# Decode attention with a long cache: keys turned in place on VectorE, block-diagonal query weights, exp before the turn of the scores, shared weight loads, fixed engine orders

## The chip, the cores and the metric

One core of one Trainium2 chip runs the whole program. The metric is the device time of one execution in microseconds (us), lower is better. Every execution that is compared below is marked fast in the record. Where times are compared, the kernels ran in the same rounds on the same chip, unless the text says that they are of different calls.

## The reference, cut to what matters

One token goes through a pre-norm block: attention over a cache of 65,536 positions with 32 query heads on 4 key/value heads, and then a gated MLP.

```python
def _A_ref(x, k_cache, v_cache, wq, wo):        # x [1,1,1024], caches [1,4,65536,128], bf16
    q = (x @ wq).reshape(B, 1, 32, 128).transpose(0, 2, 1, 3)
    k = jnp.repeat(k_cache, 8, axis=1); v = jnp.repeat(v_cache, 8, axis=1)
    p = softmax(einsum("bhqd,bhkd->bhqk", q, k) * 128 ** -0.5)
    return einsum("bhqk,bhkd->bhqd", p, v).transpose(0, 2, 1, 3).reshape(B, 1, 4096) @ wo
h  = x + _A_ref(layernorm(x), k_cache, v_cache, wq, wo)
h2 = h + (gelu(n @ w_gate) * (n @ w_up)) @ w_down      # n = layernorm(h); [1024,3584], [3584,1024]
```

Keys and values are 67 MB each and the weights 39 MB. Every byte is read once, so this is a program that loads.

## The kernel before

All large loads go through one queue into five buffers of 4 MB (32 KB in each of 128 partitions), in the order wq, K of head 0, then K of head g+1 and V of head g in turn, wo, gate, up, and the down weights in pieces of 14, 7, 4, 2 and 1 columns of 256 KB.

```python
    CW = 16384; NBUF = 5
    chpool = ctx.enter_context(tc.tile_pool(name="chpool", bufs=NBUF))
    def load(src, name):
        t = chpool.tile([P, CW], BF16, name=name, tag="ch")
        ...
        nc.sync.dma_start(out=tv, in_=src)
```

A key position lies in one partition, but the score matmul needs the 128 elements of a key across partitions. So TensorE turns pairs of bf16 as fp32 words, 128 by 128 at a time, and VectorE and ScalarE copy the result out of PSUM in turn:

```python
    # k_chunk_T, for each block b of four in a bank
    nc.tensor.transpose(out=kt_ps[:, b, :], in_=k32s[m0 // 16][:, m0 % 16, :], identity=ident_f[:])
    ...
    if act_for(g, ci, c): nc.scalar.copy(out=dst_bf, in_=src_bf)
    else:                 nc.vector.tensor_copy(out=dst_bf, in_=src_bf)
    # k_chunk_QK: four matmuls side by side on strips of 32 array columns
    for par in range(2):
        for c in range(4):
            nc.tensor.matmul(qk_ps[32 * c:32 * c + 32, :], lhsT=qsel[:, g, par, hf, :],
                             rhs=mv[:, :, 32 * c:32 * c + 32, par], ..., tile_position=(0, 32 * c))
```

The first 14 of the 28 columns of the down weights give rows in PSUM. Two neighbouring columns, each in two halves, use the four strips. The rows are copied out and summed over strips by fp32 matmuls ("row sum" below). The other 14 columns run as small matmuls with one output column, which can follow the last loads closely:

```python
    def pair_mm(bank, stat, w2, c, first, last):
        for s in range(DS):                       # two halves of 512
            g = 2 * s + c % 2
            nc.tensor.matmul(bank[32 * g:32 * g + 32, :], lhsT=stat, rhs=w2[:, s * 512:(s + 1) * 512], ...)
    def cp_sum(row, add, name):                   # the row sum: 4 fp32 matmuls
        for b in range(4):
            nc.tensor.matmul(ps[:, b, :], lhsT=row[:, b * P:(b + 1) * P], rhs=hsel[:], start=True, stop=True)
    sizes = [14, 7, 4, 2, 1]; NW = sizes[0]
    for sz in sizes:
        wv = load(wd_v[:, c0:c0 + sz, :], "wd_sb")
        for cc in range(sz):
            c = c0 + cc
            if c < NW:
                pair_mm(d_ps, actz[:, c, :], wv[:, cc, :], c, c < 2, c + 2 >= NW); continue
            for j in range(DC):
                nc.tensor.matmul(dl_ps[:, j:j + 1], lhsT=wv[:, cc, j * P:(j + 1) * P], rhs=act_bf[:, c:c + 1], ...)
        c0 += sz
        if c0 == NW: ...                          # evacuation to d_r, then cp_sum(d_r)
```

## Time and profile before

| | before |
|---|---|
| time, median of 4 (range) | 411.93 us (411.78 to 412.08) |
| span of the profiled run | 410.2 us |
| read from HBM | 173.0 MB |
| busy: PE (TensorE matmul), PEld (weight load), DVE (VectorE), ACT (ScalarE) | 66%, 47%, 41%, 40% |
| the load queue's share of 16 DMA engines' span | 98.1% |

These are lines of the profile's page of the kernel before. In the first two, busy time, share of the span and number of instructions are given by engine. The DMA row has the busy tenths of 40 equal slices of the span, and below it stands what they moved. Then come two DMA queues (packets, MB, share) and groups of instructions (busy us, mean ns of one, idle time of the engine before them, and what ended most of it).

```profile
span 410.2 us, 5998 instructions
...
PE 271.7 (66%) x2577; PEld 193.1 (47%) x2577; DVE 168.9 (41%) x292; ACT 162.9 (40%) x249; POOL 5.1 (1%) x16
...
DMA  8999999999999999999999999999999999999993
GB/s 358 412 457 407 457 408 449 419 439 428 430 436 428 439 417 451 411 449 415 447 421 439 425 428 439 427 441 427 441 424 441 428 433 425 433 441 411 446 415 163
...
q1 hardware_dynamic: 6496, 173.02, 98.1%
q8 instruction: 20, 0.33, 0.3%
...
L216 PE MATMUL kt_ps<-ident_f,k_sb 128*128 128x128 f32 x1024 | 144.5, 304 | 37.4 <-DMA k_sb<-in_A_k_cache_dram 34.4
L216 PEld LDWEIGHTS kt_ps<-ident_f,k_sb 128*128 128x128 f32 x1024 | 131.6, 158 | 58.1 <-issue 36.6
L220 ACT COPY kt_sb<-kt_ps 128x1024 bf16<-128x1024 bf16 x116 | 111.9, 1016 | 105.5 <-issue 74.8
L222 DVE COPY kt_sb<-kt_ps 128x1024 bf16<-128x1024 bf16 x140 | 95.3, 688 | 92.9 <-PE kt_ps L216 89.7
...
```

The DMA row stands at its highest digit from the second slice to the last but one. The most expensive groups all belong to the turn of the keys. There is a second queue, of kind "instruction", with 0.3%: the program's own instructions.

The next lines are of the timeline of the same run at its end (start us, duration, engine, line, operation, tiles, count, and in brackets the idle time before and its releaser). `d_ps` are the row matmuls, `hd_cp_ps` is the row sum, `dl_ps` are the small matmuls.

```profile
...
398.42 2.66 PE L353 MATMUL d_ps<-wd_sb,actz 128*32 128x512 bf16 x28 [2.72 <-DMA wd_sb<-in_B_w_down_dram]
...
401.13 0.69 DVE L461 COPY d_r<-d_ps 128x512 f32<-128x512 f32 x1 [5.20 <-PE d_ps L353]
...
401.87 1.87 PE L382 MATMUL hd_cp_ps<-hsel,d_r 128*128 128x2 f32 x8 [0.79 <-DVE d_r L461]
...
403.60 2.50 PE L456 MATMUL dl_ps<-act_bf,wd_sb 128*128 128x1 bf16 x88
...
406.32 1.01 PE L456 MATMUL dl_ps<-act_bf,wd_sb 128*128 128x1 bf16 x24 [0.21 <-DMA wd_sb<-in_B_w_down_dram]
407.37 0.17 DVE L463 TENSOR_TENSOR o_col<-dl_ps,hd_cp 128x8 bf16<-128x8 f32 x1 [3.41 <-PE dl_ps L456]
...
408.18 0.36 SPq L468 DMA_DIRECT2D out_dram<-o_row  x1
...
```

The last small matmuls wait for the last load, and the transfer of the output starts 0.85 us after they end.

### The profile page before, as it was taken

What the parts mean: (1) busy time and instruction counts of PE and PEld (TensorE: products, weight loads), DVE (VectorE), ACT (ScalarE), POOL (GpSimd) and SP (SyncE); (2) the same over time, 40 slices, a digit from 0 to 9 for tenths busy, and PEclk for the clock granted to TensorE, in tenths of its full rate; (3) what the DMA queues carried; (4) which work ended last, traced back from release to release, by engine and by line L of the source; (5) the groups of instructions that cost most, each with busy time, mean ns of one, the idle gap of its engine ahead of it and who ended that gap; (6) DMA issues with size and microseconds to landing.
All of it is one profiled execution on the core that took longest, in us unless ns stands there. A gap on an engine that the chain in (4) does not pass through costs nothing.

```text
span 410.2 us, 5998 instructions
## 1 busy us (share of the span) xinstructions
PE 271.7 (66%) x2577; PEld 193.1 (47%) x2577; DVE 168.9 (41%) x292; ACT 162.9 (40%) x249; POOL 5.1 (1%) x16
## 2 busy tenths in 40 slices
PE   0448888797994938964858399394945526467266
PEld 0227666484673727644555277182822213163135
DVE  0213787766772636751727086344630001022011
ACT  0014676597570648641525775152638000000000
POOL 1000000000000000000000000000020000000000
PEclk9986999969998886996969689979875655557665
DMA  8999999999999999999999999999999999999993
GB/s 358 412 457 407 457 408 449 419 439 428 430 436 428 439 417 451 411 449 415 447 421 439 425 428 439 427 441 427 441 424 441 428 433 425 433 441 411 446 415 163
DMA packets 6682, 173.40 MB, mean 423 GB/s; under 512 B 896, under 2 KB 896, under 8 KB 1152
## 3 DMA queue, kind: packets, MB, share of 16 engines
q1 hardware_dynamic: 6496, 173.02, 98.1%
q8 instruction: 20, 0.33, 0.3%
q14 instruction: 6, 0.05, 0.0%
q10 hardware_dynamic: 160, 0.00, 0.0%
HBM read 173.02 MB, written 0.00 MB: 422 GB/s over the span
## 4 chain that ended last, share of the span: by engine, by line
DMA 51%; PE 21%; ACT 6%; DVE 4%; issue 2%; DVEq 0%
DMA k_sb<-in_A_k_cache_dram 27%; PE kt_ps L216 13%; DMA wo_sb<-in_A_wo_dram 11%; DMA wu_sb<-in_B_w_up_dram 10%; ACT pT L272 4%; DMA wd_sb<-in_B_w_down_dram 3%; PE qk_ps L239 3%; ACT kt_sb L220 2%; PE acc_ps L289 2%; DVE mx L246 1%; PE at_ps L353 1%; PE wu_ps L158 1%; DVE kt_sb L222 1%; DVE sc_sb L245 1%; PE o_ps L305 1%
## 5 line engine op out<-in xcount | busy, mean ns | idle before, releaser
L216 PE MATMUL kt_ps<-ident_f,k_sb 128*128 128x128 f32 x1024 | 144.5, 304 | 37.4 <-DMA k_sb<-in_A_k_cache_dram 34.4
L216 PEld LDWEIGHTS kt_ps<-ident_f,k_sb 128*128 128x128 f32 x1024 | 131.6, 158 | 58.1 <-issue 36.6
L220 ACT COPY kt_sb<-kt_ps 128x1024 bf16<-128x1024 bf16 x116 | 111.9, 1016 | 105.5 <-issue 74.8
L222 DVE COPY kt_sb<-kt_ps 128x1024 bf16<-128x1024 bf16 x140 | 95.3, 688 | 92.9 <-PE kt_ps L216 89.7
L272 ACT ACTIVATE pT<-sc_sb,nbias 128x256 bf16<-128x256 f32 x64 | 47.5, 746 | 23.7 <-DVE nbias L264 23.7
L239 PE MATMUL qk_ps<-kt_sb,qsel 128*32 128x512 bf16 x512 | 39.6, 384 | 9.9 <-ACT kt_sb L220 9.2
L289 PE MATMUL acc_ps<-v_sb,pT 128*32 128x512 bf16 x512 | 37.4, 441 | 12.2 <-DMA v_sb<-in_A_v_cache_dram 12.2
L246 DVE TENSOR_REDUCE mx<-sc_sb 128x8 f32<-128x512 f32 x32 | 35.2, 1100 | 0.5
L245 DVE STREAM_TRANSPOSE sc_sb<-qk_ps 128x512 f32<-128x512 f32 x32 | 23.0, 717 | 19.0 <-PE qk_ps L239 18.7
L289 PEld LDWEIGHTS <-pT 128*32 128x32 bf16 x512 | 16.8, 107 | 28.9 <-issue 19.9
L165 ACT COPY wg_ev<-wg_ps 96x512 f32<-96x512 f32 x1 | 0.6, 582 | 59.4 <-PE wg_ps L158 59.4
L239 PEld LDWEIGHTS <-qsel 128*32 128x32 bf16 x512 | 8.3, 94 | 24.5 <-DVE kt_sb L222 15.2
L298 PE MATMUL l_ps<-lpart,ones_f 128*128 128x8 f32 x16 | 3.8, 312 | 21.7 <-ACT pT L272 21.7
L298 PEld LDWEIGHTS l_ps<-lpart,ones_f 128*128 128x128 f32 x16 | 3.2, 249 | 23.9 <-ACT pT L272 23.1
L158 PEld LDWEIGHTS <-hnz 128*32 128x32 bf16 x112 | 5.0, 127 | 17.6 <-issue 15.6
L158 PE MATMUL wu_ps<-wu_sb,hnz 128*32 128x512 bf16 x56 | 6.6, 579 | 9.3 <-DMA wu_sb<-in_B_w_up_dram 9.3
L353 PE MATMUL at_ps<-wo_sb,o2z 128*32 128x512 bf16 x64 | 7.2, 630 | 8.3 <-DMA wo_sb<-in_A_wo_dram 8.3
L272 ACT ACTIVATION_READ_ACCUMULATOR pT<-sc_sb,nbias 128x1 f32 x64 | 12.1, 190 | 0.0
L302 DVE COPY acc_sb<-acc_ps 128x512 f32<-128x512 f32 x4 | 2.7, 684 | 22.7 <-PE acc_ps L289 22.7
L165 ACT ACT_TABLE_LOAD x1 | 1.3, 1283 | 25.8 <-DVE q_ev L163 25.8
L125 PE MATMUL ln_tot<-ln_s,ones_f 128*128 128x1 f32 x4 | 1.2, 363 | 13.9 <-DVE ln_s L123 13.9
L353 PEld LDWEIGHTS <-o2z 128*32 128x32 bf16 x64 | 2.7, 140 | 12.0 <-issue 11.5
(108 smaller groups left out, 93.0 us busy)
## 6 DMA issues: line engine op xcount, KB each, us to landing
k_sb<-in_A_k_cache_dram SPq DMA_DIRECT2D x16, 4096.0 KB, 40.2
v_sb<-in_A_v_cache_dram SPq DMA_DIRECT2D x16, 4096.0 KB, 37.5
wq_sb<-in_A_wq_dram SPq DMA_DIRECT2D x2, 4096.0 KB, 16.8
wo_sb<-in_A_wo_dram SPq DMA_DIRECT2D x2, 4096.0 KB, 43.3
wg_sb<-in_B_w_gate_dram SPq DMA_DIRECT2D x2, 3584.0 KB, 43.7
wu_sb<-in_B_w_up_dram SPq DMA_DIRECT2D x2, 3584.0 KB, 40.6
wd_sb<-in_B_w_down_dram SPq DMA_DIRECT2D x1, 3584.0 KB
wd_sb<-in_B_w_down_dram SPq DMA_DIRECT2D x1, 1792.0 KB, 29.6
```

The source lines that it names most:

```text
L158: nc.tensor.matmul(banks[s // 4][32 * g:32 * g + 32, :], lhsT=stat, rhs=mov(s), start=first, stop=last, tile_position=(0, 32 * g))
L216: nc.tensor.transpose(out=kt_ps[:, b, :], in_=k32s[m0 // 16][:, m0 % 16, :], identity=ident_f[:])
L220: nc.scalar.copy(out=dst_bf, in_=src_bf)
L222: nc.vector.tensor_copy(out=dst_bf, in_=src_bf)
L239: nc.tensor.matmul(qk_ps[32 * c:32 * c + 32, :], lhsT=qsel[:, g, par, hf, :], rhs=mv[:, :, 32 * c:32 * c + 32, par], start=(hf == 0 and pa ...
L245: nc.vector.transpose(out=sl.rearrange("p n h -> p (n h)"), in_=qk_ps[:])
L246: nc.vector.tensor_reduce(out=st["mx"][:, :, pi], in_=sl.rearrange("p n h -> p h n"), axis=AX.X, op=ALU.max)
L272: nc.scalar.activation(out=pT[:, :, r, :], in_=sc_sb[:, hf * HG * TG:(hf + 1) * HG * TG, r].rearrange("p (a t) -> p a t", t=TG), func=ACT. ...
L289: nc.tensor.matmul(acc[32 * c:32 * c + rep * TG, :], lhsT=pTs[a // HG][:, a % HG, :, :].rearrange("p r t -> p (r t)"), rhs=v_sb[:, i * TG: ...
L298: nc.tensor.matmul(l_ps[:], lhsT=ones_f[:], rhs=lpart[:, hf, :], start=(hf == 0), stop=(hf == NH - 1))
L305: nc.tensor.matmul(o_ps[:], lhsT=acc_sb[:, t * Dh:(t + 1) * Dh], rhs=sel[:, t:rep * TG:TG], start=(t == 0), stop=(t == TG - 1))
L353: nc.tensor.matmul(bank[32 * g:32 * g + 32, :], lhsT=stat, rhs=w2[:, s * 512:(s + 1) * 512], start=first, stop=last, tile_position=(0, 32 ...
```

## The change

Its intent is to take TensorE, VectorE and ScalarE out of the way of the loads. VectorE turns each K load in place in blocks of 32x32 words. Query weights are laid out block-diagonally with zeros, so that TensorE scores the half-turned keys directly with the whole array. Exp runs on rows of scores that are contiguous, and only the probabilities are turned. Matmuls that use the same weights as the one before them drop the second weight load. Fixed orders on each engine take the place of the scheduler's choice. In the output stage, gate and up alternate, both halves of a column use the same strip and so share a weight load, and 21 columns instead of 14 of the down weights give rows. Buffers, load sizes and bytes are unchanged. The core of the diff, with cuts:

```diff
+    def k_load(g, li):
+        kt = kv_load(k_v[g], li, "k_sb").rearrange("p n d -> p (n d)").bitcast(U32)
+        for c in range(NSP):                                   # NSP = 4, w = 2048 words
+            dv(nc.vector.transpose(out=kt[:, c * w:(c + 1) * w], in_=kt[:, c * w:(c + 1) * w]))
...
+        for a in range(TG):
+            for bp in range(4):
+                o = W0 + (g * 4 + bp) * P - a * rep
+                for k in range(2):
+                    mm(qk_ps[:, k, :], wsel[:, o:o + P], kt[:, a, k, :, bp // 2, :, bp % 2],
+                       a == 0 and bp == 0, a == TG - 1 and bp == 3, loaded=(k == 1))
...
-                nc.tensor.transpose(out=kt_ps[:, b, :], in_=k32s[m0 // 16][:, m0 % 16, :], identity=ident_f[:])
...
+            ac(nc.scalar.activation(out=pe_r[:], in_=state.pop(("sc", g, li))[:], func=ACT.Exp, ...))
+            dv(nc.vector.transpose(out=pT[:].rearrange("p m c -> p (m c)"), in_=pe_r[:]))
...
+    def row_mm(banks, stat, w2, c, first, last):
+        g = c % 4
+        for s in range(DS):
+            mm(banks[s][32 * g:32 * g + 32, :], stat, w2[:, s * 512:(s + 1) * 512], first, last,
+               loaded=(s > 0), tile_position=(0, 32 * g))
...
     def cp_sum(row, add, name):
         for b in range(4):
-            nc.tensor.matmul(ps[:, b, :], lhsT=row[:, b * P:(b + 1) * P], rhs=hsel[:], start=True, stop=True)
+            for s in range(DS):
+                mm(ps[:, b, s:s + 1], row[:, s, b * P:(b + 1) * P], ones_f[:, 0:1], True, True)
...
-    NW = sizes[0]
+    NW = 21
```

## The prediction

> **What bounds it now.** The DMA stream. The page counts 173.0 MB read from HBM; the DMA row of the 40 slices reads 9 (90% or more busy) from the second slice to the next to last; the queue table gives the load queue 98.1% of 16 engines' span. Windows of 10 us move about 420 to 465 GB/s whatever the engines do: 426 at 310-320 us with PE busy 7.6 of 10, 419 at 330-340 with PE at 3.5 and VectorE idle. The Trainium skill ("DMA: Bandwidth & Descriptors", Specifications) gives a fabric ceiling of 435 GB/s; the trace agrees, about 431 sustained. PE (66%), VectorE (41%) and ScalarE (40%) have slack. The chain of waits shows 51% DMA and 21% PE, but its PE pieces run beside a full queue: loads are issued 40.2 us (K) before they land, at 9.7 us of stream per 4 MB load (estimate: 4.19 MB at 431 GB/s). Only the end is exposed: the last weights land near 406.95 us, the span ends at 410.2.
>
> **What the change does.** It takes out 1024 fp32 PE transposes (144.5 us busy), 256 evacuations (95.3 us VectorE, 111.9 ScalarE) and strided exps (47.5 us). It adds 64 in-place turns of 128x2048 words. Estimate: the 128x512 stream transpose takes 717 ns, so about 1.05 ns per element plus 0.18 us: 2.3 us each, 9.3 per K load. Scores and values become 512 + 512 matmuls of 512 columns on the whole array, about 0.215 us each at full clock (timeline starts), 0.427 at half: 6.9 or 13.7 us per load. Estimated busy: PE 250 us, PEld under 70, VectorE 190-200, ScalarE 40-50. Per K+V pair (19.4 us of stream) VectorE needs 11-13 us, PE 13.8; in the first head, K alone, VectorE needs about 10.5 per 9.7, which five buffers absorb. All this is off the critical path; bytes, load sizes and buffers are unchanged. Fewer instructions spare instruction fetch (0.3% of queue time): at most 0.5 us.
>
> **The end gets longer.** Before, the 14-column piece of the down weights lands at 398.4; 28 matmuls run in fours on different column strips (2.66 us), the row sum ends at 403.7, and 88+24 small matmuls follow the data. Now 21 columns go this way, and both halves of a column use one strip: about 15 slots of 0.215-0.427 us (3.2-6 us), then 8 more for the 7-column piece (estimated to land at 402.7), evacuation 0.7, row sum 1-2, then 56 small matmuls (26.7 ns apart, 1.5 us). PE then ends between 408 and 411 instead of 407.3.
>
> **Prediction.** 411.87, minus 0.3, plus 0.6 to 3.5: about 412.9 us, 80% range 411.0 to 415.5. Faster by over 2%: 2%; within 2%: 94%; slower by over 2%: 4%.
>
> **What would show it.** DMA row still 9s, load queue about 98%, same rate; last load landing within 1 us of before; K turns near 2.3 us; the last small matmuls waiting for PE, not for the last load; 4-6 us between last landing and end (3.3 before).
>
> **What would make it wrong.** Turns at two cycles per element (18 us per load) would make VectorE the bound: tens of us slower. PE held at half clock would need 27 us per pair. In-place turns could slow the DMA's writes; the skill ("SBUF — State Buffer", Who interferes with whom) says DMA ports are separate from the engines', which the constant rate supports. If the tail's small matmuls still hide behind the data, the time is 411.5.

## The result and the profile after

| | before | after |
|---|---|---|
| time, median of 4 (range) | 411.93 us (411.78 to 412.08) | 410.84 us (410.12 to 411.24) |
| span of the profiled run | 410.2 us | 409.5 us |
| last load has landed | 406.91 us | 404.18 us |
| from there to the end of the span | 3.3 us | 5.3 us |
| matmuls + weight loads on TensorE | 5154 | 2253 |

The ratio is 0.9969, 95% interval 0.9955 to 0.9983. It and all ratios below are from the fast runs of the same rounds; they are not quite the quotients of the quoted medians. The time lies 0.16 us below the low end of the predicted range: the change gave a small gain, clear of noise, where a small loss was forecast.

The lines of the page after that answer to those of before:

```profile
span 409.5 us, 2725 instructions
...
PE 307.7 (75%) x1521; PEld 70.6 (17%) x732; DVE 202.6 (49%) x189; ACT 45.5 (11%) x68; POOL 7.2 (2%) x17
...
DMA  8999999999999999999999999999999999999993
GB/s 359 410 461 410 453 416 442 427 439 432 415 451 416 455 411 451 419 448 423 439 431 426 445 414 450 419 445 423 448 423 434 435 426 445 419 432 429 439 413 151
...
q1 hardware_dynamic: 6496, 173.02, 98.1%
q8 instruction: 9, 0.15, 0.1%
...
L259 DVE STREAM_TRANSPOSE k_sb<-k_sb 128x2048 uint32<-128x2048 uint32 x64 | 142.1, 2278 | 33.8 <-DMA k_sb<-in_A_k_cache_dram 33.8
L127 PE MATMUL qk_ps<-k_sb,wsel 128*128 128x512 bf16 x256 | 104.7, 409 | 37.5 <-DVE k_sb L259 25.2
L129 PE MATMUL acc_ps<-v_sb,pT 128*128 128x512 bf16 x384 | 111.3, 401 | 0.0
...
```

The attention did what it was meant to do. The turns of the keys take 2278 ns each, weight loads fall from 193 to 71 us, ScalarE from 163 to 45 us. The load queue's share is 98.1% as before, so none of this was on the path. But the instruction queue has 9 packets instead of 20.

The end of the timeline after, with the row matmuls, the evacuation, the row sum, the small matmuls and the output:

```profile
...
395.65 0.62 PE L127 MATMUL d_ps<-wd_sb,actz 128*32 128x512 bf16 x4 [3.10 <-DMA wd_sb<-in_B_w_down_dram]
...
396.03 0.67 PE L129 MATMUL d_ps<-wd_sb,actz 128*32 128x512 bf16 x4
...
399.89 0.41 PE L127 MATMUL d_ps<-wd_sb,actz 128*32 128x512 bf16 x4 [0.91 <-DMA wd_sb<-in_B_w_down_dram]
...
400.98 0.69 DVE L216 COPY d_r<-d_ps 128x512 f32<-128x512 f32 x1 [7.95 <-PE d_ps L129]
...
401.72 3.36 PE L127 MATMUL hd_cp_ps<-ones_f,d_r 128*128 128x1 f32 x16 [0.79 <-DVE d_r L216]
...
404.95 1.63 PE L127 MATMUL dl_ps<-act_bf,wd_sb 128*128 128x1 bf16 x56
...
406.62 0.17 DVE L529 TENSOR_TENSOR o_col<-dl_ps,hd_cp 128x8 bf16<-128x8 f32 x1 [1.32 <-PE dl_ps L127]
...
407.44 0.37 SPq L534 DMA_DIRECT2D out_dram<-o_row  x1
...
```

The row matmuls start 2.8 us earlier than before: the 14-column piece was awaited until 395.65 us instead of 398.42. But now the 7-column piece gives rows too and is awaited until 399.89 us, so the evacuation starts only 0.15 us earlier (400.98 instead of 401.13). Then the row sum takes 3.36 us instead of 1.87. The small matmuls come after it in one go (the last load landed at 404.18, before they began). The end of the chain is only 0.7 us earlier.

So the question is why the loads end 2.7 us earlier, when neither their rate nor their number changed.

**Where the loads ended.** The first view is of the windows at the end of the run before: the stretch, its length, then PE, PEld, DVE, ACT and POOL busy, the granted clock, and last the DMA engines' mean busy share and GB/s.

```profile
...
402.00:403.00 1.00, 1.00 (x6) 1.00 (x6) 0.00 (x0) 0.00 (x0) 0.00 (x0) 0.50 0.70 291
403.00:404.00 1.00, 1.00 (x19) 1.00 (x20) 0.17 (x1) 0.00 (x0) 0.00 (x0) 0.50 0.54 221
404.00:405.00 1.00, 1.00 (x44) 1.00 (x42) 0.00 (x0) 0.00 (x0) 0.00 (x0) 0.50 0.55 219
405.00:406.00 1.00, 1.00 (x41) 1.00 (x38) 0.00 (x0) 0.00 (x0) 0.00 (x0) 0.50 0.27 92
406.00:407.00 1.00, 0.74 (x21) 0.57 (x19) 0.00 (x0) 0.00 (x0) 0.00 (x0) 0.50 0.08 29
...
```

The same view after:

```profile
...
402.00:403.00 1.00, 1.00 (x6) 1.00 (x7) 0.00 (x0) 0.00 (x0) 0.00 (x0) 0.50 0.68 272
403.00:404.00 1.00, 1.00 (x6) 1.00 (x6) 0.00 (x0) 0.00 (x0) 0.00 (x0) 0.50 0.34 131
404.00:405.00 1.00, 1.00 (x8) 1.00 (x8) 0.00 (x0) 0.00 (x0) 0.00 (x0) 0.50 0.00 0
405.00:406.00 1.00, 1.00 (x41) 1.00 (x41) 0.17 (x1) 0.00 (x0) 0.00 (x0) 0.50 0.00 0
...
```

Up to 402 us both run at full rate (shares of 0.97 to 1.03 in the windows from 398 us, not printed). At 402-403 us both fall to about 0.7. Before, some engines then go on for four more microseconds, with a share of about half until 405; after, they have all but stopped by 404. This is not a faster stream. It is a stream whose engines finish closer together.

The Trainium skill says in "DMA: Bandwidth & Descriptors", section "Why a DMA increments its semaphore by 16 and not by 1", that a DMA runs on up to 16 engines that finish independently and that each adds one to the completion semaphore when its data has landed. This trace agrees: each load here has 16 increments. So the first and the last of the 16 tell when the fastest and the slowest engine delivered. Read from the semaphore events of the trace:

| the last load | first increment | last increment | between |
|---|---|---|---|
| before | 402.39 us | 406.91 us | 4.52 us |
| after | 402.31 us | 404.18 us | 1.87 us |

The fastest engine is on time to within 0.1 us in both. The slowest sets the time at which a load counts as landed. Followed through the run (from the packets' own 4-byte semaphore writes), the spread between first and last grows in steps, and between the steps it is flat:

```
run      the spread over time
before   0.6 us in the first three loads; 1.6 at 41 us; 1.8 to 1.9 from 70 to 167 us; 2.9 at 177 us; 3.2 to 322 us; 4.35 at 332 us; 4.5 at 385 us
after    0.4 us in the first four loads; 1.65 at 51 us; 1.8 from 109 us to the end
```

The packets of the instruction queue, 16 KB each, start at these times (us from the span's start):

```
before   36 52 68 86 103 115 135 148 | 172 184 206 226 250 263 285 302 | 330 360 385 406
after    46 105 149 212 253 317 354 383 | 406
```

The steps follow the 1st, the 9th and the 17th packet, within a load or two. The Trainium skill, "Runtime: NRT & Kernel Launch", section "Instruction fetch mechanics", says that instruction memory is refilled in blocks of 16 KiB, 256 instructions, through a DMA queue of the sequencer's own. The counts agree: 5154 TensorE instructions before are 20.1 blocks, 2253 after are 8.8. The same section says that crossing a block boundary costs one DMA tail-bump, "mostly hidden".

**Theory A.** Each refill of TensorE's instructions costs the DMA engine that carries it about 1.2 us of loads, and refills go to eight engines in turn. The slowest engine therefore loses 1.2 us with each round of eight that has begun: three rounds before, one after (in the kernel after, the ninth refill comes at 406 us, when the loads have ended). The end of the loads is set by this engine.

**Rival B.** The loads gained from the engines' leaving the memories or the fabric alone (no transposes, less traffic on PSUM and SBUF). **Rival C.** Instruction traffic costs in proportion, some 0.25 us per refill (2.73 us over 11 refills fewer), with no rounds. A second queue of kind "instruction" on the page, q14, had six packets of 8 KB before and four after; e1 to e3 below have four as well and e5 has seven, so it is not what moves their loads' end. And for the other half of the result, the longer end: that the row sum's chain bounds it, against that the last load still does.

### The profile page after: what moved, and what is told of

Read it like the earlier page. It is cut to its first block, busy times and chain, and to the rows that moved or that the text cites. A ratio compares the mean times of both kernels' runs of the same rounds, so it can differ in the third digit from the quotient of the medians.

```text
span 409.5 us, 2725 instructions
## 1 busy us (share of the span) xinstructions
PE 307.7 (75%) x1521; PEld 70.6 (17%) x732; DVE 202.6 (49%) x189; ACT 45.5 (11%) x68; POOL 7.2 (2%) x17
## 3 DMA queue, kind: packets, MB, share of 16 engines
q1 hardware_dynamic: 6496, 173.02, 98.1%
## 4 chain that ended last, share of the span: by engine, by line
DMA 46%; PE 30%; DVE 18%; ACT 4%; issue 2%; SPq 0%; ACTq 0%; DVEq 0%
DMA k_sb<-in_A_k_cache_dram 32%; DVE k_sb L259 12%; PE acc_ps L129 10%; DMA wu_sb<-in_B_w_up_dram 8%; DMA wd_sb<-in_B_w_down_dram 6%; PE qk_ps L127 6%; PE qk_ps L129 6%; PE acc_ps L127 4%; DVE mx L280 2%; ACT sc L279 2%; DVE pT L304 1%; ACT pe_r L301 1%; PE o_ps L127 1%; DVE acc_sb L330 1%; ACT acc_sb L332 1%
## 5 line engine op out<-in xcount | busy, mean ns | idle before, releaser
L259 DVE STREAM_TRANSPOSE k_sb<-k_sb 128x2048 uint32<-128x2048 uint32 x64 | 142.1, 2278 | 33.8 <-DMA k_sb<-in_A_k_cache_dram 33.8
L127 PE MATMUL qk_ps<-k_sb,wsel 128*128 128x512 bf16 x256 | 104.7, 409 | 37.5 <-DVE k_sb L259 25.2
L129 PE MATMUL acc_ps<-v_sb,pT 128*128 128x512 bf16 x384 | 111.3, 401 | 0.0
L129 PE MATMUL qk_ps<-k_sb,wsel 128*128 128x512 bf16 x256 | 104.2, 407 | 0.0
L127 PE MATMUL acc_ps<-v_sb,pT 128*128 128x512 bf16 x128 | 51.4, 402 | 0.0
L127 PEld LDWEIGHTS <-wsel 128*128 128x128 bf16 x256 | 26.1, 102 | 143.4 <-issue 123.7
L280 DVE TENSOR_REDUCE mx<-qk_ps 128x1 f32<-128x1024 f32 x16 | 19.5, 1220 | 44.9 <-ACT sc L279 44.9
L279 ACT COPY sc<-qk_ps 128x1024 f32<-128x1024 f32 x16 | 16.2, 1012 | 201.9 <-PE qk_ps L129 201.9
L127 PEld LDWEIGHTS <-pT 128*128 128x128 bf16 x128 | 13.6, 106 | 98.3 <-issue 98.2
L304 DVE STREAM_TRANSPOSE pT<-pe_r 128x1024 bf16<-128x1024 bf16 x16 | 19.0, 1227 | 6.2 <-ACT pe_r L301 6.2
L301 ACT ACTIVATE pe_r<-sc,nbias 128x1024 bf16<-128x1024 f32 x16 | 18.2, 1140 | 14.3 <-DVE nbias L296 13.5
L127 PE MATMUL wg_ps<-wg_sb,hnz 128*32 128x512 bf16 x32 | 6.4, 591 | 3.8 <-DMA wg_sb<-in_B_w_gate_dram 3.1
```

The costliest lines, as they stand in the source:

```text
L127: return pe(t.matmul(out, lhsT=lhsT, rhs=rhs, start=start, stop=stop, tile_position=tile_position, skip_group_check=skip_group_check))
L129: op = t.add_instruction(mybir.InstMatmult(name=nc.get_next_instruction_name(), engine=t.engine, start_tensor_calc=start, stop_tensor_calc ...
L259: dv(nc.vector.transpose(out=kt[:, c * w:(c + 1) * w], in_=kt[:, c * w:(c + 1) * w]))
L279: ac(nc.scalar.copy(out=sc[:], in_=flat))
L280: dv(nc.vector.tensor_reduce(out=state[("mx", g)][:, li:li + 1], in_=flat, axis=AX.X, op=ALU.max))
L301: ac(nc.scalar.activation(out=pe_r[:], in_=state.pop(("sc", g, li))[:], func=ACT.Exp, bias=nbias[:, 0:1], scale=scale, accum_out=lpart[:, ...
```

## The experiments

Four kernels test the loads' end. They share 11 runs of the kernel before, median 412.12 us.

### Shared weight loads undone (e1_reload)

```diff
-        if not loaded:
+        if True:
             return pe(t.matmul(out, lhsT=lhsT, rhs=rhs, ...))
```

> The changed kernel with every shared weight load loaded again: 789 more TensorE instructions, otherwise the same program. Theory A (each refill of TensorE's instruction stream takes the place of about 1.2 us of loads on one DMA engine, in turn over eight engines; the slowest engine sets the end): about 12 refills instead of 9, so a second round begins: the first engine still finishes the last load near 402.3 us, the last engine at about 405.4 instead of 404.2, time about 1.2 us longer, 412.0 us. Rival B (the loads ran faster because the engines leave the memories alone): the loads' end moves by less than 0.3 us. Rival C (cost in proportion to the number of refills, 0.25 us each): plus 0.8 us.

Measured: 12 refills, first engine at 402.32, last at 405.38 us. The spread goes from 1.7 to 3.1 us with the load after the 9th refill (at 335 us). Time 411.44 us median (411.22 to 413.70), ratio to before 0.9991 (0.9975 to 1.0007), where the changed kernel had 0.9969. The loads' end moved by 1.20 us as A says. B expected a slower stream or no change, and the first engine kept its schedule while the last one fell behind. The time rose by less, 0.4 to 0.6 us between the medians of the two kernels (in different calls) and 0.7 to 0.9 us by their ratios, and it scatters. The row sum blurs it. In the profiled run of e1 it began 1.26 us later than in that of the changed kernel but took 2.15 us instead of 3.36, so that both spans are 409.5 us. In the profiled runs after and e2 the granted clock was 0.50 for nearly all of the row sum or all of it, and it took 3.36 and 3.57 us; in e1, e3 and e7 it began at full clock and took 2.15, 1.96 and 2.18. So the loads' end, not the time, is what these runs compare.

### More instructions that do nothing (e2_extra1824, e3_extra2496)

```diff
+    extra_ps = ps_x.tile([P, 512], F32, name="extra_ps")
...
+        if g < Hkv - 1:
+            for _ in range(104):          # 76 in e2
+                mm(extra_ps[0:32, 0:1], ident_bf[:, 0:32], ident_bf[:, 0:1], True, True)
```

> The changed kernel with 912 one-column matmuls into a bank nobody reads (1824 more TensorE instructions, placed after the value matmuls of the first three heads, some 2 us of TensorE each time). Theory A: 16 refills, which is the end of the second round: last engine at about 405.4 us, the same as with the weight loads repeated, time about 412.0 us. Rival B: no change in the loads' end. Rival C: plus 1.8 us, 412.6 us.

> As the run before it with 1248 one-column matmuls (2496 more instructions). Theory A: 18 refills, so a third round begins: last engine at about 406.6 us, time about 2.4 us longer than the changed kernel, 413.2 us, although only two refills more than the run before it. Rival B: no change. Rival C: plus 2.4 us over the changed kernel but only 0.5 over the run before it.

Measured for e2: 16 refills, last engine at 405.40 us, time 411.74 us (411.36 to 413.54), ratio 0.9998 (0.9985 to 1.0012). Measured for e3: 18 refills, last engine at 406.96 us, time 413.92 us (412.87 to 415.05), ratio 1.0045 (1.0033 to 1.0057). First engines: 402.32 and 402.26 us. From the page of e3:

```profile
...
PE 327.1 (80%) x2769; PEld 100.1 (24%) x1980; DVE 201.7 (49%) x189; ACT 45.5 (11%) x68; POOL 7.2 (2%) x17
...
q8 instruction: 18, 0.29, 0.3%
...
```

And its windows at the end:

```profile
...
403.00:404.00 1.00, 0.96 (x14) 0.12 (x3) 0.00 (x0) 0.00 (x0) 0.00 (x0) 0.93 0.56 229
404.00:405.00 1.00, 0.25 (x3) 0.25 (x3) 0.69 (x1) 0.59 (x1) 0.00 (x0) 1.00 0.44 176
405.00:406.00 1.00, 1.00 (x12) 1.00 (x11) 0.00 (x0) 0.00 (x0) 0.00 (x0) 1.00 0.15 61
...
```

With a program that turns keys on VectorE like the changed one, the DMA share at 404-405 us is 0.44 again, where the changed kernel had 0.00: the late engines are back. The pair of runs tells A from C. From 12 refills to 16, the last engine moved by 0.02 us (405.38 to 405.40), where C expects 1.0. From 16 to 18 it moved by 1.56 us, where C expects 0.5. The steps of the spread again come with the loads after the 9th and the 17th refill. A expected 406.6 us and a time of 413.2 for e3. Within e3 the third step is 1.2 us (3.3 to 4.6 us of spread); most of the rest is that its spread was already 0.2 us larger than that of e2 before this step.

### Fewer instructions in the kernel before (e5_before_fewer)

Wrong on purpose: half of the scores' terms and half of the values are left out. The comparison with the reference passed all the same, presumably because attention's share of the output is small against its tolerance (not tested). This is no usable kernel.

```diff
-        for par in range(2):
+        for par in range(1):
...
             c = a % 4
+            if (a // 4) % 2:
+                continue
```

> The kernel before, wrong on purpose: the odd half of the score matmuls and half of the value matmuls left out (1024 TensorE instructions fewer), everything else as it was. Theory A: 16 refills instead of 20, two rounds instead of three: the first engine finishes its last load near 402.4 us as before, the last at about 405.7 instead of 406.9, time about 1.2 us shorter, 410.7 us. Rival B: the loads' end hardly moves, since the transposes of the keys and their evacuations, most of the work beside the loads, are all still there. Rival C: minus 1.0 us.

Measured: 16 refills, first engine at 402.44, last at 405.41 us; time 410.71 us (410.61 to 410.87), ratio 0.9965 (0.9953 to 0.9977). Its windows at the end:

```profile
...
404.00:405.00 1.00, 1.00 (x44) 1.00 (x41) 0.00 (x0) 0.00 (x0) 0.00 (x0) 0.50 0.53 201
405.00:406.00 1.00, 0.83 (x28) 0.73 (x25) 0.13 (x1) 0.00 (x0) 0.00 (x0) 0.50 0.01 4
...
```

The last engine ends 1.5 us earlier than in the kernel before (shares of 0.53 and then 0.01, where before had 0.55, 0.27 and 0.08). All 1024 transposes and 256 evacuations are still there. Leaving out four refills, and with them a third round, gave about as much as the whole change did. This run alone would not tell A from C. Together with e1 to e3 it says that the number of rounds sets the loads' end in both programs.

The packets in the ten kept traces show rounds and price more directly than these comparisons. Packets of one DMA engine stand back to back, so the load packet that starts where a refill's packet ends (within 0.03 us) is taken to be of the same engine. In the ten traces, 128 refills have such a load packet behind them; the others come after or just before the loads' end. These refills' packets took 0.88 to 0.97 us. The load packet behind took 1.67 to 1.76 us where those of 32 KB usually take 1.21, or 1.52 to 1.61 where those of 28 KB take 1.06. Together a refill costs its engine 1.43 us (1.42 to 1.46), more than the 1.2 of A.

The rounds show as well. In every run with more than eight refills before the loads' end, the refills' packet times repeat after eight to within 0.01 us, while within a round they differ by up to 0.09 us. And the 16 increments of the last load stand in groups. Before, seven come within 1.1 us of the first, six 2.6 to 3.1 us after it and three 4.25 to 4.5 us, near twice and three times 1.43: 19 refills in turn over eight engines visit five of them twice and three of them three times. After, nine come 1.4 to 1.9 us after the first, where eight refills visit eight engines once. In each of these two runs one engine more is late than the refills account for; the other instruction queue may be the reason (not tested).

### Which part of the change gives and which takes (e6_new_attention, e7_new_output)

The next four kernels ran in another call and share 11 runs of before, median 412.04 us. The changed kernel was run again with them. e6 is the changed file up to the end of attention followed by the old output stage, e7 the reverse; the diff is where the two files are joined.

> The changed kernel again, beside the others of this call on the same chip. Expected: 410.8 us with a spread of about 1 us, eight refills before the end, last engine at about 404.2 us, some 5.3 us from there to the end of the span.

> The new attention with the output stage of the kernel before (its pairing of strips, its row sum of four matmuls, 14 columns in rows and 14 columns as small matmuls, gate before up). Theory A: nine refills, the ninth close to the end: last engine at 404.2 us if the ninth comes too late to matter, 405.4 if it comes in time; from there to the end as in the kernel before (3.3 us), so 409.2 or 410.4 us. Rival (the gain of the change came from its output stage): 411.9 us as before.

> The attention of the kernel before with the new output stage. Theory A: 19 or 20 refills, third round, last engine at about 406.9 us as before, and the longer chain at the end: the 7-column piece lands at about 402.6, TensorE ends at 408 to 409.5, time 412.5 to 414. Rival (the gain of the change came from its output stage): 410.8 us.

| | refills | last load landed | time, median (range) | ratio to before (95%) |
|---|---|---|---|---|
| e8, the changed kernel again | 9 | 404.16 us | 411.02 us (409.92 to 412.31) | 0.9974 (0.9959 to 0.9988) |
| e6, new attention, old output | 9 | 404.31 us | 409.45 us (409.37 to 409.68) | 0.9938 (0.9925 to 0.9951) |
| e7, old attention, new output | 19 | 406.95 us | 413.87 us (412.59 to 414.06) | 1.0034 (1.0022 to 1.0046) |

The two parts work against each other. Attention with fewer instructions gives 2.6 us, the new output stage costs 1.8 us, and the sum of the two (-0.8) is near what the whole change measured (-1.0). In e6 the ninth refill came at 403.7 us, too late to matter, so the first branch of its expectation held. The end of e6:

```profile
...
399.76 1.87 PE L440 MATMUL hd_cp_ps<-hsel,d_r 128*128 128x2 f32 x8 [0.79 <-DVE d_r L519]
...
401.49 3.25 PE L514 MATMUL dl_ps<-act_bf,wd_sb 128*128 128x1 bf16 x112
...
404.77 0.17 DVE L521 TENSOR_TENSOR o_col<-dl_ps,hd_cp 128x8 bf16<-128x8 f32 x1 [2.93 <-PE dl_ps L514]
...
```

The row sum of four calls takes 1.87 us and runs before the small matmuls need TensorE; 112 small matmuls end 0.43 us after the last landing (the next step starts at 404.77).

### The row sum in one pass (e4_bf16sum)

```diff
-            d_r = rows.tile([P, DS, 512], F32, name="d_r")
+            d_r = rows.tile([P, DS, 512], BF16, name="d_r")
...
-            hd_cp = cp_sum(d_r, h_cp, "hd_cp")
+            hd_cp = cp_sum(d_r, h_cp, "hd_cp", one_bf)       # a column of ones in bf16
```

> The changed kernel with the rows of the down projection kept in bfloat16, so that the row sum is eight one-pass matmuls instead of sixteen fp32 ones (3.36 us in the profile). Theory A (in the changed kernel the end is bound by the chain from the 7-column piece: matmuls, evacuation, row sum, small matmuls): the row sum takes under 0.7 us, the small matmuls follow the data again, TensorE ends at about 404.4 us instead of 406.6, time about 408.9 us. Rival (the last load bounds the end): no change, 410.8 us.

Measured: 409.43 us (409.29 to 409.56), ratio 0.9936 (0.9924 to 0.9948), correct; TensorE ended at 404.7 us, and the time is 0.5 us above what was expected. The same part of its timeline:

```profile
...
402.18 0.35 PE L127 MATMUL hd_cp_ps<-one_bf,d_r 128*128 128x1 bf16 x8 [0.80 <-DVE d_r L216]
...
402.41 0.95 PE L127 MATMUL dl_ps<-act_bf,wd_sb 128*128 128x1 bf16 x32
...
403.68 1.00 PE L127 MATMUL dl_ps<-act_bf,wd_sb 128*128 128x1 bf16 x24 [0.31 <-DMA wd_sb<-in_B_w_down_dram]
...
404.72 0.17 DVE L531 TENSOR_TENSOR o_col<-dl_ps,hd_cp 128x8 bf16<-128x8 f32 x1 [1.98 <-PE dl_ps L127]
...
```

The row sum takes 0.35 us instead of 3.36, and the last 24 small matmuls again wait for their load (the bracket in the third line). The loads themselves ended at 404.26 us, as in the changed kernel. So the chain through the row sum cost the changed kernel about 1.6 us (411.02 to 409.43), and its scatter with it: the range of e4 is 0.27 us, that of the changed kernel in the same rounds 2.4 us. e4 and e6 reach the same time (409.43 and 409.45 us) by different ways, because in both the chain to the output follows the end of the loads.

## Why the prediction was right or wrong

- **What bounds the kernel: right.** The load queue stayed at 98.1%. Turns of 2.28 us (2.3 predicted), ScalarE at 45 us and VectorE at 203 us came out at or near the estimates, TensorE at 308 us instead of 250, and none of it mattered. That in-place turns do not slow the DMA's writes, which the prediction took from the Trainium skill's "SBUF — State Buffer", section "Who interferes with whom", also held: the fastest engine ended at 402.31 us with them and at 402.39 without.
- **"Fewer instructions spare instruction fetch (0.3% of queue time): at most 0.5 us": this is the step that failed.** The cost was named, and its size was wrong: the loads ended 2.73 us earlier, more than five times the limit given and nine times the 0.3 us that the sum used. The estimate took a share of 16 engines' time, as if the refills were spread evenly over them. The runs show that refills come in rounds over eight engines, that each costs its engine 1.43 us, and that a load has landed only when the slowest engine has delivered. Spread evenly, eleven refills fewer at 1.43 us would give 1.0 us (estimate from these numbers); the slowest engine was spared two of its three, 2.9 us, and 2.73 were measured. The expectation "last load landing within 1 us of before" fell with it.
- **"The end gets longer": right in sum, not in its terms.** From the last landing to the end, 4 to 6 us were predicted, and 5.3 measured; the output stage alone costs 1.8 us (e7), inside the predicted 0.6 to 3.5. The sum came right by luck, because two terms were mis-sized in opposite directions. "About 15 slots (3.2-6 us)" for the 14-column piece measured 3.3 us at a granted clock of 0.50, where the estimate's own arithmetic gives about 6: the 28 matmuls start in 8 groups, not 15. Four matmuls on four strips start within 15 ns of each other (395.653 to 395.668), although the two halves of a column stand next to each other in the program's source. And "row sum 1-2" was 3.36 us, because two banks make eight fp32 calls instead of four, which the page counts as 16 matmuls where before it counted 8, and because the clock was 0.50 (about 2.0 to 2.2 us where it began at full clock).
- **"The last small matmuls waiting for PE, not for the last load": right**, as e4 shows by taking the row sum away.
- **The sum.** 411.87 - 0.3 + (0.6 to 3.5) became, in the two profiles, 410.2 - 2.7 + 2.0 = 409.5. With the first term as predicted (-0.3), the same end would have fallen inside the range.

What stays open: the trace does not number DMA engines, so that refills visit eight of them in turn is read from the steps after the 1st, 9th and 17th refill, from packet times that repeat after eight, and from the groups of late increments. Why the load packet behind a refill takes about 0.5 us longer, so that 16 KB cost 1.43 us on an engine that carries 32 KB of K or V in 1.21 us, is not settled. Nor is the 0.3 to 0.7 us of spread before the first refill.

## What to carry to other kernels

When loads keep all DMA engines busy, the slowest engine sets the time, and a share averaged over 16 engines hides it: compare the first and the last of a load's 16 semaphore increments before you call the stream full. Count the instructions of the longest instruction stream in blocks of 256, since in these runs the blocks fetched while the loads run were paid in rounds; taking out instructions can pay where taking out work does not. And price the few microseconds after the last load as a chain of its own: there two serial microseconds are two microseconds.

## What the Trainium skill lacked or had wrong

- "Runtime: NRT & Kernel Launch", Instruction fetch mechanics: the cost of crossing a 16 KiB boundary is not hidden for a program bound by its loads. Each refill cost the DMA engine that carried it 1.43 us, and the slowest engine fell behind with the 1st, 9th and 17th (last landing at 404.2, 405.4 and 407.0 us with 9, 12 to 16, and 18 refills in the program; the ninth of the 9 came after the loads' end). That refills go in turn over some of the engines is in no page.
- "DMA: Bandwidth & Descriptors": it says that a DMA's engines finish independently, but not how far apart they can drift under a full queue. Here it was 4.5 us at the end of the run of the kernel before (4.7 in e3), with the fastest engine on the same schedule to within 0.3 us in all runs (402.26 to 402.54 us for the last load).
- "TensorE: Matmul & The Clock Gate", Part 2, says that matmuls stay in program order. In the trace after, the second half of a column, next in the program's source, started 0.38 us after the first, and the first halves of the next three columns started before it (395.653, then 395.658 to 395.668, then from 396.031 us), each on its own strip. The helper `pe` fixes the source's order on TensorE; that the instruction stream kept it was not read out. The 28 matmuls took 3.3 us at a granted clock of 0.50.
